# Batch 0's down-sampled attention in blocks of 128 and 16 queries, with four smaller edits around it

## Chip, core and metric

The kernel runs on one core of one Trainium2 chip. The metric is the device time of one execution in microseconds; the median of several runs is given. A core has TensorE (PE in the profile: matmuls; PEld are its weight loads), VectorE (DVE), ScalarE (ACT), GpSimd (POOL) and SyncE (SP), each with its own queue of instructions in program order. Semaphores order them against each other and against the DMAs.

## What is computed

Two stages. The first is attention over inputs `q`, `k`, `v` of shape (8 batches, 8 heads, 576 positions, 64). For each batch and head two attentions are added: one over means of four neighbouring positions (144 of them, its output repeated four times), and one in which a query sees only keys less than four positions away:

```python
q_d = q.reshape(B, H, Sd, factor, D).mean(axis=3)      # k_d, v_d alike; factor 4, Sd 144
out_d = sm_attn(q_d, k_d, v_d)
out_up = np.repeat(out_d, factor, axis=2)
mask = np.abs(pos[:, None] - pos[None, :]) < factor
scores = np.where(mask, scale * np.matmul(q, k.transpose(0, 1, 3, 2)), -1000000000.0)
out_local = np.matmul(softmax(scores), v)
return out_up + out_local
```

(`softmax` stands here for the five lines of the reference that spell it out.) The second stage takes the result as `x`, 4608 tokens of 512 values, through two matrix products with a gate between them:

```python
h = x @ w_in                                           # w_in 512 x 2048
g = h * (1.0 / (1.0 + np.exp(-1.702 * h)))
return (g @ w_out).astype(np.float32)                  # w_out 2048 x 512
```

## The kernel before

**Tiles and stages.** The second stage is cut into nine groups of 512 tokens. A group has `mm1` (16 blocks of 128 columns of `w_in`, four matmuls each, line L703, then a Silu on ScalarE, L714) and `mm2` (64 matmuls, L759, or a split form for the last tokens). The attention of batch g + 1 is cut into steps, and the lists `POS` and `POS_0` name the block of group g before which each step is issued on TensorE; `POS_0` is for group 0, whose steps belong to batch 1, and `VDP_0` places `prep_vd_pe(1, ...)`. So attention and matrix products share TensorE in an order written out by hand; nothing is scheduled automatically.

**The start.** Batch 0's attention has nothing to hide behind. It is a straight list of calls after line L797: loads, constants, `warm` (matmuls of zeros in fp32, L656; each appears in the trace as two records), `scores` (L384) and `scores_d` (L403, down-sampled) of two quads of heads, their exponentials on ScalarE (`exp_local` L414, `exp_down` L420), then for each of four head pairs `av_local0` (L523), `av_down0` (L539) and `normalise0` on VectorE (L558 to L565), then `transp_sum` (L580 and L591), which transposes the result and adds the up-sampled part, and `copy_x` (L604 to L610) into `xT`. The partial products of group 0's first six column blocks (`part`, L703) stand between the transposes.

**Sums of v.** Batch 0's down-sampled values are made on TensorE by `prep_vd_pe` (L346) in three chunks: the first two with one copy on ScalarE (L355), the third with another. The third is issued after `scores_d(0, 1, PA[2])`; so ScalarE has that copy, and then `exp_down(1, sd)`, in its queue. PSUM tile `PA[2]` holds the second down-scores until `exp_down` has read them, and is then the output tile of the third head pair.

**`av_down0`** takes, for each head pair, ten blocks of up to 64 queries, each for two heads: 20 matmuls with 48 rows (positions), 64 columns of weights and 65 columns of values (64 and a column that sums). Down-sampled queries 0 to 47, 48 to 95 and 96 to 143 lie in three places of the output tile.

**`up`** is a 0/1 matrix by which `transp_sum` repeats each down-sampled query four times. It is made of a difference of indices (iotas on GpSimd, L113 to L116) by Abs and Exp on ScalarE (`make_up`), with a bias that `make_bias` computes on VectorE. `mask` (used for batches 1 to 7 at L428) is spread out on ScalarE by `make_mask` after the third head pair.

**Queues.** GpSimd's queue issues most loads (q, k, v of batches 0 and 1, the weights) and does iotas, sums and memsets between them. A wait at one of these holds all that is behind it. After the start it holds, in this order: `load_w_out(1)`, the memset of `v4` (L888), `load_vb(1, 0)`, `load_vb(1, 1)`, the pooling of batch 1. SyncE issues the loads of later batches and the stores.

Of the kernel before, what the change touches and what calls it, by code (L numbers as in the profile page):

```python
# [8 lines left out]
FP32 = mybir.dt.float32  # L9
BF16 = mybir.dt.bfloat16  # L10
AF = mybir.ActivationFunctionType
# [8 lines left out]
def kernel(  # L20
# [9 lines left out]
    nc = tc.nc  # L30
    B, H, S, D = q.shape
    SD = S // 4
# [14 lines left out]
    consts = ctx.enter_context(tc.tile_pool(name="consts", bufs=1))  # L47
    persist = ctx.enter_context(tc.tile_pool(name="persist", bufs=1))
# [7 lines left out]
    id128 = consts.tile([128, 128], BF16, name="id128")  # L56
# [4 lines left out]
    vbs = [persist.tile([128, 5, H, 65], BF16, name=f"vb{i}") for i in range(2)]  # L61
    vds = [persist.tile([128, 3, HP, 65], BF16, name=f"vd{i}") for i in range(2)]
    es = [persist.tile([128, 2, 304], BF16, name=f"es{i}") for i in range(4)]
    eds = [persist.tile([128, 2, 464], BF16, name=f"ed{i}") for i in range(2)]
    v4 = persist.tile([128, 3, HP, 4 * D], FP32, name="v4")
    kdT = [persist.tile([128, 160, 2], BF16, name=f"kdT{i}") for i in range(NQ)]

# [1 line left out]
    PM = [psum.tile([128, 512], FP32, name=f"pm{i}") for i in range(2)]  # L69
# [9 lines left out]
        turn["m"] += 1  # L79
        return PM[turn["m"] % 2]  # L80

    UP = 120
    wz = consts.tile([128, 512], FP32, name="wz")
    off = consts.tile([128, 60], BF16, name="off")
    psel = consts.tile([128, 7, 64], BF16, name="psel")
# [5 lines left out]
    di = consts.tile([128, 128], FP32, name="di")  # L91
    dr = consts.tile([128, 1], FP32, name="dr")
    du = consts.tile([128, UP], FP32, name="du")
    bias = consts.tile([128, 4], FP32, name="bias")
    dp = consts.tile([128, 7, 64], FP32, name="dp")
    it = dict(allow_small_or_imprecise_dtypes=True)
    halves = [slice(0, 64), slice(64, 128)]
# [13 lines left out]
        nc.gpsimd.iota(di, pattern=[[-1, 128]], base=0, channel_multiplier=1, **it)  # L111

    def iota_up():  # L113
        for par in range(2):
            nc.gpsimd.iota(du[halves[par]], pattern=[[1, UP]], base=-48 * par,
                           channel_multiplier=-1, **it)  # L116

    def fill():
        nc.vector.memset(wz, 0.0)
        for t in kdT:  # L120
            nc.vector.memset(t[:, SD:160, :], 0.0)
        for t in vbs:
            nc.vector.memset(t[:, :, :, 64:65], 1.0)
        for t in vds:
            nc.vector.memset(t[:, :, :, 64:65], 4.0)
        for t in es:
            nc.vector.memset(t[:, :, 300:304], 1.0)
        for t in eds:
            nc.vector.memset(t[:, :, 432:464], 1.0)


    def make_off():
# [4 lines left out]
        )  # L137

    def make_mask():
        nc.scalar.copy(  # L140
            out=mask.rearrange("p x (i c) -> p (x i) c", c=60),
            in_=dm[:, None, :].to_broadcast([128, 10, 60]),
        )
# [5 lines left out]
        nc.vector.tensor_single_scalar(out=id128, in_=di, scalar=0.0, op=ALU.is_equal)  # L149

    def make_bias():
        nc.vector.memset(bias[:, 3:4], -3.0)
        nc.vector.reduce_sum(
            out=bias[:, 2:3], in_=id128.rearrange("p (h c) -> p h c", h=2)[:, :, 0:48],
            axis=mybir.AxisListType.XY,
        )
        nc.vector.tensor_copy(out=bias[:, 0:2], in_=rv)
        nc.vector.tensor_scalar(
            out=bias[:, 0:3], in0=bias[:, 0:3], scalar1=-1.0, scalar2=400.0,
            op0=ALU.add, op1=ALU.mult,  # L160
        )

    def make_up():
        nc.scalar.activation(out=du, in_=du, func=AF.Abs)
        nc.scalar.activation(
            out=up, in_=du[:, :, None].to_broadcast([128, UP, 4]),
            func=AF.Exp, scale=-400.0, bias=bias[:, 2:3],
        )

    rv = consts.tile([128, 2], FP32, name="rv")  # L170
# [14 lines left out]

    def end_psel():
        nc.scalar.activation(out=dp, in_=dp, func=AF.Abs)
        nc.scalar.activation(out=dp, in_=dp, func=AF.Relu, bias=bias[:, 3:4])
        for sl, c in ((slice(0, 1), 1), (slice(1, 7), 0)):
            nc.scalar.activation(  # L190
                out=psel[:, sl], in_=dp[:, sl],
                func=AF.Exp, scale=-400.0, bias=bias[:, c : c + 1],
            )
# [201 lines left out]
    def scores_d(b, qd, sd=None):  # L395
        sd = sd or ps_tile()
        bank = banks(sd)
        for kc in range(3):
            for a in range(2):
                for r in range(4):  # L400
                    rows = slice(32 * r, 32 * r + 32)
                    j = r % 2
                    nc.tensor.matmul(  # L403
                        bank[r // 2][64 * j : 64 * j + 64, SD * kc : SD * kc + SD],
                        lhsT=kdT[qd][rows, 48 * kc : 48 * kc + 64, a],
                        rhs=qdT[b, qd][rows, :, a],
                        start=(a == 0), stop=(a == 1),
                        tile_position=(32 * r, 64 * j),
                    )
        return sd  # L410
# [119 lines left out]

    def av_down0(hp, o):
        Ed, vd, u = eds[hp // 2], vds[0], hp % 2
        blocks = [(0, 3)] + [(kc, c) for kc in range(3) for c in (0, 1)]
        blocks += [(kc, 2) for kc in range(3)]
        for kc, c in blocks:
            pos, slot = ((0, 6), (1, 6), (1, 4), (1, 5))[c]
            for j in range(2):
                q0 = SD * kc + 48 * c if c < 3 else 0
                nc.tensor.matmul(  # L539
                    o[64 * pos : 64 * pos + 64, j, 65 * slot : 65 * slot + 65],  # L540
                    lhsT=Ed[64 * j : 64 * j + 48, u, q0 : q0 + 64],
                    rhs=vd[64 * j : 64 * j + 48, kc, hp, :],
                    start=(kc == 0), stop=(kc == 2 or c == 3),
                    tile_position=(64 * j, 64 * pos),
                )

    def y_tiles0():
        return (
# [20 lines left out]

    def transp_sum(y, x):  # L570
        y, yd = y[:2]
        ups = [
            (0, 6, sub(x[0], 3, (1, 228)), sub(up, 3, (228, 2), (1, 114))),
            (0, 6, sub(x[0], 0, (1, 3)), sub(up, 0, (1, 3))),
            (0, 4, sub(x[0], 231, (1, 117)), sub(up, 267, (1, 117))),
            (1, 6, sub(x[1], 3, (1, 228)), sub(up, 117, (228, 2), (1, 114))),
            (1, 4, sub(x[1], 156, (1, 75)), sub(up, 192, (1, 75))),
        ]
        for n, (bank, slot, to, what) in enumerate(ups):
            nc.tensor.matmul(  # L580
                to, lhsT=yd[:, slot // 2 - 2, :, :], rhs=what,
                start=n in (0, 3), stop=True,
                skip_group_check=True,
            )
# [14 lines left out]
        return x  # L599
# [53 lines left out]
    def warm(n, cols=512, t=None):  # L653
        t = pm_tile() if t is None else t
        for _ in range(n):
            nc.tensor.matmul(  # L656
                t[:, 0:cols], lhsT=wz[:, 0:128], rhs=wz[:, 0:cols], start=True, stop=True
            )

    def attention(b, slots=None):  # L660
        st = {}
# [124 lines left out]
            f()  # L786

    POS = [13, 16, 33, 42, 53, 62, 71]
    POS_0 = [16, 18, 27, 46, 50, 55, 64, 68, 73]
    VDP_0 = 41  # L790

    o, y, x = {}, {}, {}

# [33 lines left out]
    prep_1("q", 0, 1)  # L827
    reduce_qk(0, 1, "k")
    reduce_qk(0, 1, "q")
    warm(3)  # L830
    exp_down(0, scores_d(0, 0, PA[2]))
    make_up()
    sp = scores(0, 1, barred=True, sp=PA[0:2])
# [6 lines left out]
    for hp in range(2):  # L840
        av_local0(hp, o[hp], range(4))
        normalise0(o[hp], y[hp], "a")
    sd = scores_d(0, 1, PA[2])
    prep_vd_pe(0, PM[1], range(2, 3))
    exp_down(1, sd)
    nc.scalar.preload_act_table_set("silu_and_others")
    for hp in range(3):
        av_local0(hp, o[hp], range(4 if hp < 2 else 0, 5))
        av_down0(hp, o[hp])
        normalise0(o[hp], y[hp], "b" if hp < 2 else "ab")  # L850
    warm(1, t=PM[0])
    make_mask()

    gT0 = new_gT()
# [103 lines left out]
```

## Time and profile before

| | |
|---|---|
| median of 5 runs | 328.76 us (325.86 to 330.29) |
| the profiled execution, its own time | 328.37 us |
| its span, first to last instruction | 326.4 us |
| mean granted TensorE clock | 0.990 |
| VectorE, ScalarE, GpSimd busy | 41%, 57%, 43% of the span |
| matmuls of the second stage, L703 and L759 | 121.5 and 121.7 us busy |
| first scores matmul (L384), first partial product (L703), end of the partial products | 8.35, 26.36, 33.6 us |
| group 1's first `mm1` matmul | 66.3 us |

The profile is of one execution. Its page gives, for each engine, the share of the span in which it was busy, the chain of work that ended last, and the costliest groups of instructions by line. The trace behind it can be asked for the waits of an engine (which instruction waited, and for whom), for the instructions in order of time, and for the busy times and the granted TensorE clock in any stretch. "<-issue" means that the profile shows nothing that the instruction waited for. Time in which an engine other than the bounding one idles costs nothing by itself.

### The profile page before, as it was taken

The page shows a single profiled execution, that of the slowest core. Times are in us where ns is not written, and L with a number is a line of the kernel's source. Part 1 is how long each engine was busy: PE and PEld are TensorE (multiplying, and loading weights), DVE is VectorE, ACT ScalarE, POOL GpSimd, SP SyncE. Part 2 cuts the span into 40 slices and gives each one's busy share as a digit, 9 for nine tenths or more (in the row PEclk, how much of TensorE's full clock was granted, in tenths as well). Part 3 has the DMA queues.
Part 4 walks back from the last instruction along what each step waited for, and adds up shares of the span by engine and source line. Part 5 has one row for each costly group of instructions (what it writes and reads, how often), then busy time and mean ns, then how long its engine had stood idle before and what let it go on. Part 6 is the DMA issues. An engine that isn't in the chain of part 4 may idle for free.

```text
span 326.4 us, 11056 instructions
## 1 busy us (share of the span) xinstructions
PE 316.1 (97%) x4954; PEld 158.2 (48%) x4954; DVE 132.9 (41%) x221; ACT 185.1 (57%) x321; POOL 139.0 (43%) x171
## 2 busy tenths in 40 slices
PE   8979979999999999999999999999999999999996
PEld 3545444445554555455544554455444544444444
DVE  6864422760477037803681277226730560000000
ACT  4443873465936593559366746674567556415611
POOL 8983950069505960497029801990098000000000
PEclk9978999999999999999999999999999999999999
DMA  7999999989716991599139922995190100021012
GB/s 124 122 195 210 165 139 214 186 216 184 147 50 150 194 192 39 145 197 204 44 98 222 182 86 89 186 205 109 66 145 3 68 34 34 0 75 56 0 55 74
DMA packets 63550, 40.02 MB, mean 123 GB/s; under 512 B 44048, under 2 KB 54416, under 8 KB 63504
## 3 DMA queue, kind: packets, MB, share of 16 engines
q1 hardware_dynamic: 44496, 24.32, 34.6%
q0 software_dynamic: 18864, 14.95, 31.9%
q8 instruction: 38, 0.62, 0.8%
q14 instruction: 8, 0.07, 0.1%
q10 hardware_dynamic: 144, 0.07, 0.1%
HBM read 44.83 MB, written 9.44 MB: 166 GB/s over the span
## 4 chain that ended last, share of the span: by engine, by line
PE 91%; DMA 2%; issue 2%; POOL 2%; ACT 1%; DVE 1%; POOLq 0%; DVEq 0%
PE pm L703 36%; PE pm L759 36%; PE pa L384 3%; PE pa L703 2%; DMA qb<-in_q_dram 2%; PE pa L759 2%; PE pa L403 2%; PE pa L498 2%; PE pa L445 2%; PE pa L467 2%; PE pm L774 1%; DVE y L484 1%; POOL vb L233 1%; PE pm L656 1%; PE pa L508 0%
## 5 line engine op out<-in xcount | busy, mean ns | idle before, releaser
L759 PE MATMUL pm<-w_out_bf,gT 128*128 128x512 bf16 x528 | 121.7, 380 | 0.0
L703 PE MATMUL pm<-xT,w_in_bf 128*128 128x512 bf16 x544 | 121.5, 380 | 0.0
L714 ACT ACTIVATE gT<-pm 128x512 bf16<-128x512 f32 x136 | 81.1, 598 | 44.9 <-PE pm L703 44.8
L703 PEld LDWEIGHTS <-w_in_bf 128*128 128x128 bf16 x576 | 55.7, 98 | 66.8 <-issue 0.4
L759 PEld LDWEIGHTS <-gT 128*128 128x128 bf16 x560 | 51.5, 98 | 59.1 <-issue 0.2
L428 DVE TENSOR_TENSOR es<-es,mask 128x600 bf16<-128x600 bf16 x28 | 19.9, 725 | 92.0 <-ACT es L414 91.2
L309 POOL TENSOR_TENSOR pq<-kT 128x576 f32<-128x576 bf16 x14 | 16.2, 1156 | 95.2 <-DVE kT L279 95.2
L744 ACT ACTIVATE osb<-pm 128x512 f32<-128x512 f32 (+2 forms) x35 | 20.8, 593 | 40.2 <-PE pm L759 36.4
L617 ACT COPY od<-pa 128x384 f32<-128x384 f32 (+1 forms) x56 | 18.5, 412 | 30.8 <-DVE y L484 22.4
L484 DVE TENSOR_TENSOR y<-pa,rc 128x896 bf16<-128x896 f32 x28 | 30.6, 1092 | 1.0
L638 DVE TENSOR_TENSOR xT<-pa,od 128x570 bf16<-128x570 f32 x28 | 21.1, 753 | 10.6 <-ACT od L617 9.8
L746 DVE TENSOR_SCALAR osb<-pm 128x128 f32<-128x128 f32 x1 | 0.3, 292 | 55.3 <-ACT osb L744 55.3
L325 POOL TENSOR_TENSOR v<-v 112x512 f32<-112x512 f32 x18 | 22.8, 1264 | 0.0
L414 ACT ACTIVATE es<-pa 128x600 bf16<-128x600 f32 x32 | 19.7, 667 | 2.8 <-PE pa L384 2.6
L279 DVE STREAM_TRANSPOSE kT<-kb 128x576 f32<-128x576 f32 x16 | 19.9, 1246 | 0.0
L279 DVE STREAM_TRANSPOSE qT<-qb 128x576 f32<-128x576 f32 x16 | 19.8, 1237 | 0.0
L233 POOL DMA_DIRECT2D vb<-in_v_dram x20 | 13.7, 702 | 6.5 <-DMA w_in_bf<-in_moe_w_in_dram 4.0
L420 ACT ACTIVATE ed<-pa 128x864 bf16<-128x864 f32 x16 | 14.4, 897 | 3.7 <-PE pa L403 3.7
L384 PEld LDWEIGHTS <-kT 32*64 32x64 bf16 x1280 | 11.7, 104 | 6.7 <-issue 5.3
L309 POOL TENSOR_TENSOR pq<-qT 128x576 f32<-128x576 bf16 x13 | 14.9, 1146 | 0.0
L483 DVE RECIPROCAL rc<-pa 128x14 f32<-128x14 f32 x28 | 6.7, 240 | 19.9 <-PE pa L467 19.9
L328 POOL TENSOR_TENSOR vd<-v 112x256 bf16<-112x256 f32 x18 | 13.6, 758 | 1.4
(97 smaller groups left out, 270.4 us busy)
## 6 DMA issues: line engine op xcount, KB each, us to landing
out_dram<-osb SPq DMA_DIRECT2D x35, 256.0 KB, 2.1
vf<-in_v_dram SPq DMA_DIRECT2D x60, 128.0 KB, 5.8
v<-in_v_dram SPq DMA_DIRECT2D x36, 192.0 KB, 4.9
kb<-in_k_dram POOLq DMA_DIRECT2D x16, 288.0 KB, 6.9
qb<-in_q_dram POOLq DMA_DIRECT2D x16, 288.0 KB, 8.2
w_out_bf<-in_moe_w_out_dram POOLq DMA_DIRECT2D x4, 512.0 KB, 13.1
vb<-in_v_dram POOLq DMA_DIRECT2D x20, 64.0 KB, 5.5
w_in_bf<-in_moe_w_in_dram POOLq DMA_DIRECT2D x2, 512.0 KB, 7.0
```

The lines of the kernel that those rows point to most:

```text
L279: nc.vector.transpose(out=t32.rearrange("p (i c) -> p c i", c=18), in_=store[b, qd].bitcast(FP32).rearrange("p (c d) -> p c d", c=18),)
L309: nc.gpsimd.tensor_tensor(out=t1, in0=sv[:, :, 0:2, :], in1=sv[:, :, 2:4, :], op=ALU.add)
L325: eng.tensor_tensor(out=t1[0:112], in0=x[:, :, 0:2, :], in1=x[:, :, 2:4, :], op=ALU.add)
L384: nc.tensor.matmul(sp[r // 2][64 * par : 64 * par + 64, r % 2, 60 * i : 60 * i + 60], lhsT=kT[b, qd][rows, k0 : k0 + 64, a], rhs=qT[b, qd] ...
L414: nc.scalar.activation(out=es[2 * qd + u][:, :, 0:300], in_=sp[u][:, :, 0:300], func=AF.Exp, scale=inv_sqrt_d,)
L428: nc.vector.tensor_tensor(out=ev, in0=ev, in1=mask, op=ALU.mult)
L484: nc.vector.tensor_tensor(out=y[:, xs], in0=ov[:, :, :, 0:D], in1=rc[:, xs].to_broadcast([128, n, 7, D]), op=ALU.mult,)
L638: eng.tensor_tensor(out=sub(xT[hp], t0 + 3, (57, 2), (114, 5), (1, 57)), in0=sub(x, 3, (509, 2), (57, 5), (1, 57)), in1=sub(od, 3, (57, 2) ...
L703: nc.tensor.matmul(acc, lhsT=w_in_bf[:, dmc, ffc * 128 : (ffc + 1) * 128], rhs=xT[dmc][:, g * TG : g * TG + TG], start=(dmc == 0), stop=(d ...
L714: nc.scalar.activation(out=gT[:, ffc, :], in_=acc, func=AF.Silu, scale=GELU_SCALE)
L744: eng.activation(out=osb, in_=ap, func=AF.Copy, scale=1.0 / GELU_SCALE)
L759: nc.tensor.matmul(ops[t], lhsT=gT[:, ffc, t * 128 : (t + 1) * 128], rhs=w_out_bf[:, ffc, :], start=(ffc == 0), stop=(ffc == n_ffc - 1),)
```

## The change

`av_down0` takes 128 queries in one block and the last 16 in another: 12 matmuls for 20. The second block's values are repeated, so that one matmul with 130 columns fills two slots of the output. The layout of `up`, its iotas, the bias and the five up-sampling matmuls of `transp_sum` follow. The third chunk of `prep_vd_pe` is issued before the second `scores_d`. `make_mask` runs on GpSimd. The three fp32 warming matmuls before the first `scores_d` become 22 bf16 matmuls with 256 columns, and the fp32 warming matmul after the third head pair is removed. Batch 1's steps from the fourth on are placed two blocks later, and `VDP_0` three.

```diff
-    UP = 120
+    UP = 144
...
     def iota_up():
-        for par in range(2):
-            nc.gpsimd.iota(du[halves[par]], pattern=[[1, UP]], base=-48 * par,
-                           channel_multiplier=-1, **it)
+        nc.gpsimd.iota(du[:, 0:128], pattern=[[1, 128]], base=0,
+                       channel_multiplier=-1, **it)
+        nc.gpsimd.iota(du[:, 128:UP], pattern=[[1, UP - 128]], base=64,
+                       channel_multiplier=-1, **it)
...
     def make_mask():
-        nc.scalar.copy(
+        nc.gpsimd.tensor_copy(
...
     def make_bias():
-        nc.vector.memset(bias[:, 3:4], -3.0)
-        nc.vector.reduce_sum(
-            out=bias[:, 2:3], in_=id128.rearrange("p (h c) -> p h c", h=2)[:, :, 0:48],
-            axis=mybir.AxisListType.XY,
-        )
+        nc.vector.memset(bias[:, 2:3], -3.0)
...
         nc.scalar.activation(
             out=up, in_=du[:, :, None].to_broadcast([128, UP, 4]),
-            func=AF.Exp, scale=-400.0, bias=bias[:, 2:3],
+            func=AF.Exp, scale=-400.0,
         )
...
     def av_down0(hp, o):
         Ed, vd, u = eds[hp // 2], vds[0], hp % 2
-        blocks = [(0, 3)] + [(kc, c) for kc in range(3) for c in (0, 1)]
-        blocks += [(kc, 2) for kc in range(3)]
-        for kc, c in blocks:
-            pos, slot = ((0, 6), (1, 6), (1, 4), (1, 5))[c]
-            for j in range(2):
-                q0 = SD * kc + 48 * c if c < 3 else 0
-                nc.tensor.matmul(
-                    o[64 * pos : 64 * pos + 64, j, 65 * slot : 65 * slot + 65],
-                    lhsT=Ed[64 * j : 64 * j + 48, u, q0 : q0 + 64],
-                    rhs=vd[64 * j : 64 * j + 48, kc, hp, :],
-                    start=(kc == 0), stop=(kc == 2 or c == 3),
-                    tile_position=(64 * j, 64 * pos),
-                )
+        for p0, n, q0, slots in ((0, 128, 0, (6, 7)), (64, 64, 128, (4, 6))):
+            for kc in range(3):
+                for j in range(2):
+                    c0, c1 = 65 * slots[0], 65 * slots[1]
+                    nc.tensor.matmul(
+                        o[p0 : p0 + n, j, c0:c1],
+                        lhsT=Ed[64 * j : 64 * j + 48, u, SD * kc + q0 : SD * kc + q0 + n],
+                        rhs=vd[64 * j : 64 * j + 48, kc, hp, None, :].to_broadcast(
+                            [48, slots[1] - slots[0], 65]
+                        ),
+                        start=(kc == 0), stop=(kc == 2),
+                        tile_position=(64 * j, p0),
+                    )
...
             (0, 6, sub(x[0], 0, (1, 3)), sub(up, 0, (1, 3))),
-            (0, 4, sub(x[0], 231, (1, 117)), sub(up, 267, (1, 117))),
+            (0, 6, sub(x[0], 231, (1, 53)), sub(up, 459, (1, 53))),
+            (0, 4, sub(x[0], 284, (1, 64)), sub(up, 512, (1, 64))),
             (1, 6, sub(x[1], 3, (1, 228)), sub(up, 117, (228, 2), (1, 114))),
-            (1, 4, sub(x[1], 156, (1, 75)), sub(up, 192, (1, 75))),
...
+    zero16 = wz.bitcast(BF16)[:, 0:256]
...
-    POS_0 = [16, 18, 27, 46, 50, 55, 64, 68, 73]
-    VDP_0 = 41
+    POS_0 = [16, 18, 27, 48, 52, 57, 66, 70, 75]
+    VDP_0 = 44
...
     reduce_qk(0, 1, "q")
-    warm(3)
+    for n in range(22):
+        nc.tensor.matmul(
+            PM[1][:, 0:256], lhsT=zero16[:, 0:128], rhs=zero16, start=True, stop=True
+        )
     exp_down(0, scores_d(0, 0, PA[2]))
...
+    prep_vd_pe(0, PM[1], range(2, 3))
     sd = scores_d(0, 1, PA[2])
-    prep_vd_pe(0, PM[1], range(2, 3))
     exp_down(1, sd)
...
         normalise0(o[hp], y[hp], "b" if hp < 2 else "ab")
-    warm(1, t=PM[0])
     make_mask()
```

The tiles `eds` grow from 464 to 480 columns, and the columns that `fill` sets to 1 with them.

More of the change, by code (lines that the diff above doesn't have):

```diff
@@ L63 @@
     es = [persist.tile([128, 2, 304], BF16, name=f"es{i}") for i in range(4)]
-    eds = [persist.tile([128, 2, 464], BF16, name=f"ed{i}") for i in range(2)]
+    eds = [persist.tile([128, 2, 480], BF16, name=f"ed{i}") for i in range(2)]
     v4 = persist.tile([128, 3, HP, 4 * D], FP32, name="v4")
@@ L93 @@
     du = consts.tile([128, UP], FP32, name="du")
-    bias = consts.tile([128, 4], FP32, name="bias")
+    bias = consts.tile([128, 3], FP32, name="bias")
     dp = consts.tile([128, 7, 64], FP32, name="dp")
@@ L128, in fill @@
         for t in eds:
-            nc.vector.memset(t[:, :, 432:464], 1.0)
+            nc.vector.memset(t[:, :, 432:480], 1.0)
     def make_off():
@@ L151, in make_bias @@
     def make_bias():
-        nc.vector.memset(bias[:, 3:4], -3.0)
-        nc.vector.reduce_sum(
-            out=bias[:, 2:3], in_=id128.rearrange("p (h c) -> p h c", h=2)[:, :, 0:48],
-            axis=mybir.AxisListType.XY,
-        )
+        nc.vector.memset(bias[:, 2:3], -3.0)
         nc.vector.tensor_copy(out=bias[:, 0:2], in_=rv)
         nc.vector.tensor_scalar(
-            out=bias[:, 0:3], in0=bias[:, 0:3], scalar1=-1.0, scalar2=400.0,
+            out=bias[:, 0:2], in0=bias[:, 0:2], scalar1=-1.0, scalar2=400.0,
             op0=ALU.add, op1=ALU.mult,
@@ L187, in end_psel @@
         nc.scalar.activation(out=dp, in_=dp, func=AF.Abs)
-        nc.scalar.activation(out=dp, in_=dp, func=AF.Relu, bias=bias[:, 3:4])
+        nc.scalar.activation(out=dp, in_=dp, func=AF.Relu, bias=bias[:, 2:3])
         for sl, c in ((slice(0, 1), 1), (slice(1, 7), 0)):
@@ L581, in transp_sum @@
                 to, lhsT=yd[:, slot // 2 - 2, :, :], rhs=what,
-                start=n in (0, 3), stop=True,
+                start=n in (0, 4), stop=True,
                 skip_group_check=True,
```

## The prediction

> **What bounds the kernel now.** I read the page first, then the waits of TensorE, its timeline, and the busy times and clock by stretches.
>
> ```profile
> span 326.4 us, 11056 instructions
> ...
> PE 316.1 (97%) x4954; PEld 158.2 (48%) x4954; DVE 132.9 (41%) x221; ACT 185.1 (57%) x321; POOL 139.0 (43%) x171
> ...
> q8 instruction: 38, 0.62, 0.8%
> ```
>
> TensorE is the bound: busy 97% of the span and 91% of the chain that ended last. From 66 us on the chain is almost only its matmuls. Whatever the change brings must come from the first 66 us. Who does TensorE wait for there?
>
> ```profile
> PE pa L403 <- issue: 2.3, 1, 2.3
> PE pa L539 <- issue: 1.5, 1, 1.5
> ```
>
> Columns: us in total, times, longest. These are the two large waits, and both are "issue": no semaphore ended them. The timeline of TensorE shows the second one and what follows:
>
> ```profile
> 18.51 0.40 PE L539 MATMUL pa<-vd,ed 48*64 48x65 bf16 x20
> 19.16 0.35 PE L523 MATMUL pa<-vb,es 64*64 64x65 bf16 x19 [0.25 <-ACT ed L420]
> ...
> 19.35 0.22 PE L539 MATMUL pa<-vd,ed 48*64 48x65 bf16 x3
> 21.10 0.49 PE L539 MATMUL pa<-vd,ed 48*64 48x65 bf16 x15 [1.53 <-issue]
> 21.52 2.07 PE L656 MATMUL pm<-wz 128*128 128x512 f32 x2
> 23.39 0.78 PE L580 MATMUL pm<-up,yd 128*128 128x228 bf16 x5
> ```
>
> TensorE stops five matmuls into `av_down0` of the third head pair, with all operands there, stands from 19.57 to 21.10, runs the other 15, then the warming matmul (L656), then `transp_sum`. The stretches (TensorE busy and count, weight loads, VectorE, ScalarE, GpSimd, granted clock, DMA share, GB/s):
>
> ```profile
> 17.24:20.65 3.41, 1.86 (x97) 1.23 (x89) 2.93 (x9) 2.68 (x4) 2.98 (x5) 1.00 1.16 181
> 20.65:27.48 6.83, 6.38 (x92) 3.71 (x92) 3.07 (x6) 2.19 (x7) 2.72 (x2) 0.50 1.14 212
> 44.55:47.96 3.41, 2.30 (x95) 1.24 (x92) 1.42 (x3) 2.88 (x5) 0.80 (x2) 1.00 1.17 178
> ```
>
> After the stop the clock is 0.50 until 27.5. The stop thus costs its 1.53 us and half the speed of 6.83 us after it.
>
> [...]queue q8 moved 38 packets, 0.62 MB, 16 KB each[...]. Counting matmul records from 0, the two waits end at record 351 and at 735: 384 apart, three blocks of 128 matmuls. [...]these two cost 1.53 and 2.25 us. The packet records of q8 show how: TensorE entered the block before (record 223) at 16.22, the packet ran from 18.23 to 19.60, matmuls resumed 1.50 later. For record 735: entered at 42.77, packet 46.86 to 47.80, resumed 1.31 later. So a block comes 2.0 to 4.1 (queueing[...]) + 0.9 to 1.6 (packet) + 1.5 us after the previous one is entered, and stops TensorE when its 128 small matmuls take less. [...]0.50 for 6.83 us, two windows, after one that was 55% busy; the stretch from 44.55, 67% busy, kept 1.00.
>
> **The change part by part.** *Counts of instructions.* Up to the stop the change adds 22 bf16 matmuls, removes the three fp32 ones (six records) and removes eight in each of the two `av_down0` before it: 22 - 6 - 16 = 0. The boundary stays five matmuls into the third `av_down0`. But the one before it, record 223, comes after the warming (+16) and ahead of any `av_down0`: it moves from the first `av_local0` (16.22) to the second half of the next `warm(1)`, about 14.2. The fetch that was late is asked for 2.0 us earlier. With the same 2.0 + 1.4 + 1.5 it is usable at 19.1; the boundary is reached at about 19.2 (below). I take it that the stop goes; the bounds are queueing of 0.6 us (usable 17.7) and 4.1 us (21.2, stop as before).
>
> *Third sum chunk ahead of the down-scores.* Four L346 matmuls (0.36 us) go before 24 of L403 (0.51). Their data, the last `vb` transfer, landed at 16.27, before 16.98 where they now start. The ACT queue has CAST `vd` (17.95 to 18.33) and then exp (18.21 to 19.11) in the same order; now the cast runs about 17.45 to 17.8, while TensorE does L403, and exp 17.95 to 18.85: 0.26 us earlier. Behind exp wait the third `av_local0` (bank `PA[2]`) and the table load. The four L346 delay L403 by 0.36, less than the cast took away.
>
> *`av_down0`.* 20 matmuls become 12 with 1170 columns for 1300. Batch 1's four heads' worth of the same kind, 80 matmuls (lines L445 and L467), ran from 60.76 to 61.33, so 8 fewer are 0.06 us; [...]I take 0.05 gained. `transp_sum`: five as before, 576 columns for 651, 0.03 us each at full clock.
>
> *Mask.* ACT loses 0.69 us at 20.42, where it then idles to 24.61. On GpSimd a cast of 2560 elements took 2.34 us, so 600 take 0.55; the two-input 576 took 1.15: 0.5 to 1.2 us. Behind it in the POOL queue: memset `v4` (2.65 us), one `vb` issue at 23.15, then a wait of 4.0 us until 27.86 for a `w_in` DMA. The cover is that wait; VectorE reads the mask only at 44.89. Cost 0.
>
> *Warming.* Six fp32 records ran from 9.12 to 11.89. 512 columns of bf16 take 0.216 us (0.43 a pair), so 22 of 256 take 2.4; L403 waits for `qdT` (VectorE, 11.67) anyway. [...]The fp32 warming at 21.52 goes: -2.00 us[...].
>
> *Small ones.* Iotas 0.22 + 0.24 become about 0.25 + 0.14 (rows L111, L110), -0.07; `make_up` does 576 columns for 480, +0.1 by the row of 600 in 0.67. Together 0, on the path (exp of scores at 15.46). The reduce on VectorE (0.25) and larger memsets lie beside waits for `kb`, `qb`: 0.
>
> *After the stop.* Walking TensorE on at full clock: third pair done 19.45; `transp_sum` 0 (0.97 at half clock, now 0.55) to 20.0; fourth pair to 20.5; `transp_sum` 1 to 21.05; the first partial matmuls wait for ACT's copies (table load ends 20.1, then 0.98 a copy), 0.15; `transp_sum` 2 waits for VectorE's third normalise (21.85), 0.2; `transp_sum` 3 for the fourth (23.43), 0.4; the remaining 18 at 0.216. The end of the partial matmuls moves from 33.61 to 27.9. Cross-check: 1.53 + 2.00 + half of 4.4 us of work at half clock + 0.26 + 0.2 - 0.75 of these waits = 5.4. I take 5.5.
>
> *Will batch 1's data be there?* Landings (from the records): last `w_in` 27.57, `qb` of batch 1 30.4 and about 33, `w_out` parts 35.7, 38.7, 48.9, 50.8, last `vb` 44.36. Needed after the change: ffc 8 at 29.6, down-scores at 37.0 (GpSimd's sums end 35.8), second part at 39.4, `vb` at 46.4 (three steps later than now), third at 49.3. All fit, by 0.4 to 2 us. The moved steps cost 0.1: the last merge then ends 0.05 before its reader, now 0.48.
>
> *The stop at 49.11.* Its boundary (18 records later in the program) falls behind two L759, 0.56 later than now after the previous one: 2.25 becomes 1.7, with queueing from 1 to 4.1 us 0 to 2. Take -0.5.
>
> **Sum:** 5.5 + 0.5 - 0.1 = 5.9. Span 326.4 - 5.9 = 320.5; the profiled execution's time is 1.97 above its span, so 322.5; it lay 0.4 below the median of the runs (328.76), so 322.8.
>
> **Rivals.** *Half clock anyway (16%)*: the stop goes, but TensorE still idles near 15.6, 16.6 and 18.6 (0.27 + 0.23 + 0.4)[...]. Against: that is under 35% of 3.41, and 33% idle was borne at 44.55. Loss up to half of 6.83 less waits that it fills: 2.9, so 325.7. *The stop stays (14%)*: queueing of 4 us at record 223. Then only the warming is won, 2.00 less what the half clock eats of it later, 0.86 to 1.4 with the rest: 327.5. *Slower (10%)*: one mechanism, at record 95. Its crossing moves from 10.51 to about 9.4, record 223 from 16.22 to 14.2; the block must be usable by 14.2, so its packet must start by 11.3. Above 1.9 us of queueing (0.62 was measured there) TensorE stops there too; at 4.1 it stands 2.3 us, enters the next block at 16.5, stops at 351 until 21.5 to 23[...]: +3, 331.5. *The change does nothing* would need the wait not to be the fetch; the 384 speaks against it, and I count that under the second.
>
> **Chances.** Main case 60%: 322.8, from 319.8 (no stop at 735 either, 2 us, and the runs' own scatter) to 325. The range takes in the first two rivals: 319.8 to 327.8, leaving out the slower case and a little. Over 1% (3.3 us, about what can be told from no change) faster: 0.60 + half of 0.16 + some of the second = 0.72; within 0.18; slower 0.10.
>
> **What would show it.** No "issue" wait at L539; a q8 packet starting near 16 and not 18.2; clock 1.00 from 20 to 28; exp of the second down-scores ending near 18.85; the partial matmuls ending near 28; 1 to 2 us still lost near 43, now at L759. Wrong: a q8 packet that starts after 17.5, a clock of 0.50 anywhere, TensorE waiting for `vb` or `w_out` of batch 1.

## The result, and the profile after

The changed kernel took 325.15 us (median of 43 runs, 321.8 to 330.07); the kernel before, run beside it on the same chips, 326.2 us (80 runs, 323.67 to 331.06). The ratio is 0.9954 with a 95% interval from 0.9936 to 0.9971: 1.5 us faster where 5.9 us were forecast. (The ratio leaves out, for both kernels, the runs that took over 1.5% more than the fastest one; the two medians are of all runs, and lie 1.05 us apart.) 322.8 was the forecast time; 325.15 lies inside the stated range, but the size of the change is a quarter of the forecast. And the kernel before itself came out at 326.2, 2.6 us below the median of the five runs that the forecast started from (the 80 take these five in).

The profiled execution took 325.43 us, 2.9 less than the profiled one of before. Its page:

```profile
span 323.7 us, 11019 instructions
...
PE 315.9 (98%) x4936; PEld 159.3 (49%) x4936; DVE 134.0 (41%) x220; ACT 184.4 (57%) x320; POOL 139.5 (43%) x172
...
q8 instruction: 38, 0.62, 0.8%
```

18 matmuls fewer (16 more in the warming, 32 fewer in `av_down0`, the two records of the late warming gone), as counted. The waits of TensorE (us in total, times, longest):

```profile
PE pa L464 <- issue: 1.1, 1, 1.1
PE pa L442 <- issue: 0.6, 1, 0.6
PE pa L534 <- issue: 0.5, 1, 0.5
```

The wait in `av_down0` (now L534) shrank from 1.5 to 0.5, and the 2.3 of batch 1's down-scores is gone. But two others have come: 1.1 us in batch 1's products (L464, at 58.7 us) and 0.6 us in those of a later batch (120 us). The timeline of TensorE around the third head pair:

```profile
18.92 0.26 PE L534 MATMUL pa<-vd,ed 48*128 48x65 bf16 x5
19.72 0.48 PE L534 MATMUL pa<-vd,ed 48*128 48x65 bf16 x7 [0.54 <-issue]
20.13 0.45 PE L577 MATMUL pm<-up,yd 128*128 128x228 bf16 x5
```

The stop is again five matmuls into `av_down0`, at record 351, and `transp_sum` follows at once, without the warming. The stretches (columns as before the change; the granted clock is the third figure from the end):

```profile
13.97:17.38 3.41, 2.90 (x72) 1.53 (x70) 2.29 (x6) 2.88 (x6) 3.41 (x8) 1.00 1.16 122
17.38:20.79 3.41, 2.87 (x95) 1.99 (x85) 2.94 (x9) 2.27 (x3) 1.10 (x2) 1.00 1.20 193
20.79:27.62 6.83, 6.83 (x87) 3.80 (x83) 2.62 (x5) 2.60 (x9) 4.74 (x4) 0.50 1.13 212
```

Here is the surprise: after 3.41 us in which TensorE was 84% busy by the trace the clock was 0.50 all the same, for 6.83 us, as before. (The trace's complete records of the granted clock last 13.653, 6.827 and 296.960 us here, 13.653, 6.827 and 300.373 before: 4, 2, 87 and 88 times 3.413. A 3.413 us piece of them is called a window.) The end of the partial products came at 31.7 us, not at 27.9.

**The granted clock sorts the runs.** Each run's mean clock is given with its time, and it takes steps: 1.000, 0.995, 0.989, 0.984. One window of 3.41 us at half clock is half of 3.41 in 324, or 0.005, so each step is taken for one such window (the profiled execution, with 6.83 us at 0.50, has a mean of 0.989). Counting them so (203 runs of the kernel before, from three sessions of the experiments below, without the 27 of a fourth, one of which took 528.23 us at a clock of 0.56; 44 of the changed kernel):

| half-clock windows in a run | before: share, median us | changed: share, median us |
|---|---|---|
| 0 | 28%, 324.8 | 36%, 323.2 |
| 1 | 39%, 326.3 | 23%, 324.8 |
| 2 | 30%, 329.3 | 32%, 326.0 |
| 3 or more | 3%, 331.3 | 9%, 329.1 |

The profile that the prediction was read from was one with two windows. From two windows to none is 329.3 to 323.2, 6.1 us, close to the 5.9 that were forecast. But the change doesn't take the windows away (1.2 a run after, 1.1 before); it is worth 1.6 us in runs without them and 3.3 in runs with two. Nor is the clock all that these runs differ in: two windows at half clock can take at most 3.4 us, and the kernel before is 4.5 us slower with two than with none. What the rest is stays open.

### The profile page after: what moved, and what is told of

Same layout as the page of the kernel before. It is cut to its first block, busy times and chain, and to the rows that moved or that the text cites. A ratio compares the mean times of both kernels' runs of the same rounds, so it can differ in the third digit from the quotient of the medians.

```text
span 323.7 us, 11019 instructions
## 1 busy us (share of the span) xinstructions
PE 315.9 (98%) x4936; PEld 159.3 (49%) x4936; DVE 134.0 (41%) x220; ACT 184.4 (57%) x320; POOL 139.5 (43%) x172
## 4 chain that ended last, share of the span: by engine, by line
PE 91%; DMA 2%; ACT 2%; POOL 2%; issue 1%; DVE 1%; POOLq 0%; DVEq 0%
PE pm L702 37%; PE pm L758 35%; PE pa L381 3%; PE pa L702 2%; PE pa L758 2%; DMA qb<-in_q_dram 2%; PE pa L400 2%; PE pa L442 2%; PE pa L495 2%; PE pa L464 2%; PE pm L773 1%; ACT es L411 1%; PE pa L534 1%; POOL vb L230 1%; PE pa L577 1%
## 5 line engine op out<-in xcount | busy, mean ns | idle before, releaser
L306 POOL TENSOR_TENSOR pq<-kT 128x576 f32<-128x576 bf16 x14 | 16.2, 1158 | 89.8 <-DVE kT L276 89.8
## 6 DMA issues: line engine op xcount, KB each, us to landing
w_out_bf<-in_moe_w_out_dram POOLq DMA_DIRECT2D x4, 512.0 KB, 14.2
```

Source lines behind the costliest of these rows:

```text
L306: nc.gpsimd.tensor_tensor(out=t1, in0=sv[:, :, 0:2, :], in1=sv[:, :, 2:4, :], op=ALU.add)
```

## Experiments

Theories: the half-clock windows come from the stop for an instruction block (*stop*, the prediction's), or from how little of the array the small matmuls use (*array use*), and the prediction's profile was one *draw* among several. Then: which parts of the change carry the 1.6 us. Each kernel was timed in five rounds unless said otherwise. Records are matmuls counted from 0. In the trace of before the first twelve packets of q8 (16,384 bytes each, the page's "instruction") start 0.62 to 4.09 us after records 95, 223, 351 and so on, every 128, and its two long issue waits end at 351 and 735; these records are called the boundaries of instruction blocks.

### b_again: the kernel before once more

No edit.

> The kernel before, unchanged, profiled once more. Theory 'draw': the waits for instruction blocks at records 351 and 735 and the half-clock windows differ from execution to execution, and the profile that the prediction was made from was a bad one. Then this profile has other lengths for the two waits (sum clearly below the 3.8 us of before), and the granted clock of its runs falls into steps of about 0.005 (one window of 3.41 us at half clock is 1.7 of 325), with times that follow: about 324 without a window, 326 with two. Theory 'fixed': the two waits are again 1.5 and 2.3 us and nearly all runs have a clock of 0.990.

Median 325.82 us (22 runs), ratio 0.9992 (0.9962 to 1.0023); 9 runs had no window, 7 one, 4 two, 2 three. This profile is of a run at full clock, and its waits are others:

```profile
PE pa L539 <- issue: 1.2, 1, 1.2
PE pa L467 <- issue: 1.0, 2, 0.8
PE pa L384 <- DVE qT L279: 0.9, 1, 0.9
PE pa L445 <- issue: 0.5, 1, 0.5
```

1.2 us at record 351 and, at 735, 0.16 where the first profile had 2.25; instead 0.8 and 0.5 at records 863 and 991. With the 1.2 us at 351 the clock stayed at 1.00 here. So 'draw' holds: two executions of one kernel waited 1.5 and 1.2 us at the same record 351, and 2.25 and 0.16 at 735. What is missing at 735 stands at 863 and 991, where the first profile had no wait; that the one leads to the other is not shown.

### a_latewarm: the late warming put back

```diff
         normalise0(o[hp], y[hp], "b" if hp < 2 else "ab")
+    warm(1, t=PM[0])
     make_mask()
```

> The changed kernel with the fp32 warming matmul after the third head pair put back (two records). Theory 'the warming was pure cost': 0.9 us slower than the changed kernel at full clock, up to 2.0 in half-clock runs, and the clocks spread as in the changed kernel. Rival 'it holds the clock': a run has fewer half-clock windows with it (more runs at 1.0), and the median is no slower than the changed kernel's 325.2.

Median 326.35 (22 runs). In the nine runs without a window 323.94, 0.76 above the changed kernel's 323.18; windows 1.5 a run, so it doesn't hold the clock. Its price in the changed kernel is near what its two records take at full clock (0.96 us from their start to that of the next matmul, in this profile), less than half of the 2.00 that the prediction read off a half-clock profile.

### a_fp32: three fp32 warmings for the 22 bf16 ones

```diff
-    for n in range(22):
-        nc.tensor.matmul(
-            PM[1][:, 0:256], lhsT=zero16[:, 0:128], rhs=zero16, start=True, stop=True
-        )
+    warm(3)
```

> The changed kernel with the three fp32 warming matmuls in place of the 22 bf16 ones: 16 records fewer ahead of everything. Theory 'block boundary': record 223 falls 16 records later in the program (into the first local product, about 15.9 us instead of 14.2), its fetch starts about 1.7 us later, and record 351 (now the last records of the third head pair, or behind it) is waited for 1.5 to 2.2 us instead of 0.5. Later boundaries move too. Rival 'the warming only warms': the wait stays at 0.5 us, and the time is that of the changed kernel within 0.3 us.

The boundaries moved as counted: record 223 was crossed at 16.22 us in the first local product, and 351 fell into `transp_sum` (L588) at 20.53. But the wait there was 0.17 us, not 1.5 to 2.2: the packet came 2.05 us after the crossing, took 0.97, and matmuls resumed 1.28 later, while the later boundary was itself reached 1.2 us later (20.36 for 19.19). A miss in size. The time without windows, 323.26 (11 of 16 runs), is the changed kernel's. So the bf16 warming brought no gain that can be seen. It may even cost windows: with the fp32 matmuls there were 0.44 a run for 1.2, and the median of all runs is 323.60, a ratio to before of 0.9919 (0.9890 to 0.9949), where the changed kernel has 0.9954 (0.9936 to 0.9971). The intervals overlap and the sessions differ, so this is a hint and not a result.

### a_busy, a_small, a_busy4: full and small matmuls ahead of the third head pair

```diff
     for hp in range(3):
+        if hp == 2:
+            for n in range(8):
+                nc.tensor.matmul(
+                    PM[0][:, 0:256], lhsT=zero16[:, 0:128], rhs=zero16,
+                    start=True, stop=True,
+                )
         av_local0(hp, o[hp], range(4 if hp < 2 else 0, 5))
```

`a_small` has `lhsT=zero16[0:32, 0:64], rhs=zero16[0:32, :]` into 64 partitions instead, as many matmuls of as many columns on an eighth of the array. `a_busy4` has four of the full ones.

> The changed kernel with eight bf16 zero matmuls (128 x 128 weights, 256 columns, 0.87 us of the full array) before the third head pair, where TensorE waits for the exponential. By the trace TensorE was 84% busy in the window before the clock fell (17.4 to 20.8), so busy time by the trace doesn't decide. Theory 'array use': [...]the head pairs' 64 x 65 tiles count little (about 0.2 of the window), and with 0.87 us of full matmuls added it stays above what it stayed above from 44.5 us on. Then nearly all runs have a clock of 0.995 to 1.0, the profile shows 1.00 from 20.8 to 27.6, and the time is 1 to 2 us below the changed kernel's median in spite of 0.5 us more on TensorE. Theory 'stop': the clock falls because TensorE stands at record 351 (now inside these eight matmuls or just after them); then the clocks spread as in the changed kernel, and the time is 0.5 us above it.

> The control of a_busy: the same eight matmuls of 256 columns in the same place, but with 32 rows and 64 columns of weights, an eighth of the array; as many records, as long in time. Theory 'array use': the clock falls as in the changed kernel (about 1.2 windows a run, a third of the runs without any), median about 325. Theory 'time busy' (TensorE must only be kept running, with whatever): as a_busy, nearly all runs at full clock, median 323.4.

> a_busy with four matmuls instead of eight, 0.43 us of the full array. Theory 'array use' with a threshold: between a_busy (0.05 windows a run) and the changed kernel (1.2); I expect 0.2 to 0.7 windows, median 323.2 to 324.2. If already four hold the clock in nearly all runs, the median is at most a_busy's 323.4, as they end before the exponential that the third pair waits for.

| | runs | without a window | windows a run | median us | median without windows |
|---|---|---|---|---|---|
| changed kernel | 44 | 16 | 1.2 | 325.0 | 323.2 |
| a_small | 24 | 10 | 1.25 | 325.1 | 322.8 |
| a_busy4 | 16 | 14 | 0.12 | 322.9 | 322.9 |
| a_busy | 20 | 19 | 0.05 | 323.4 | 323.1 |

(The changed kernel's row has one run, of 324.4 us, more than the 43 above; hence 325.0.) The control decides: with the same time on TensorE (1.06 and 1.05 us for the eight, in the two profiles) there were 1.25 windows a run with the small tile and 0.05 with the full one. Keeping TensorE running wasn't enough here.

Where do the windows lie in a profile? The records of the clock start and change whole multiples of 3.413 us apart (the lengths above), so each profile's windows can be counted from its own. They lie differently in each: one begins at 17.38 us in the profile of the changed kernel, at 18.48 in that of `a_busy4`. The windows of `a_busy4` around the head pairs:

```profile
15.07:18.48 3.41, 2.86 (x86) 1.87 (x83) 2.07 (x5) 2.97 (x6) 3.41 (x7) 1.00 1.08 152
18.48:21.90 3.42, 3.42 (x105) 2.48 (x98) 3.01 (x9) 2.34 (x4) 1.81 (x3) 1.00 1.22 205
21.90:25.31 3.41, 3.36 (x55) 2.13 (x53) 1.78 (x4) 1.97 (x9) 3.30 (x2) 1.00 1.12 213
```

of `a_small`'s profiled run:

```profile
16.20:19.57 3.37, 3.13 (x102) 2.14 (x97) 2.41 (x7) 2.86 (x5) 2.70 (x6) 1.00 1.21 195
19.57:22.98 3.41, 2.17 (x47) 1.64 (x45) 1.13 (x5) 0.57 (x1) 3.35 (x3) 1.00 1.19 214
22.98:29.60 6.62, 6.40 (x83) 3.63 (x82) 3.03 (x6) 2.60 (x9) 2.43 (x4) 0.50 1.11 211
```

and of `b_again`, the kernel before in a run at full clock:

```profile
15.71:19.12 3.41, 2.78 (x135) 1.97 (x134) 2.54 (x7) 2.60 (x5) 2.65 (x5) 1.00 1.16 180
19.12:22.54 3.42, 2.28 (x72) 1.50 (x71) 2.51 (x7) 1.76 (x3) 3.38 (x2) 1.00 1.17 199
```

In `a_small`'s profile TensorE also stood 1.24 us at record 351, in the window before the fall, so that profile alone doesn't tell 'stop' from 'array use'; the counts of runs do.

An estimate of array use, worked out from the traces: a matmul's columns at 0.216 us for 512 (the rate of L703), times rows and weight columns over 128 x 128. Up to 66 us the windows at full clock after which the clock fell had 0.28 (changed kernel, from 17.4), 0.20 (before), 0.19 (`b_nowarm`), 0.18 and 0.07 (`a_small`) and 0.12 (`b_pos`). The lowest after which it stayed had 0.28 (`a_busy4_pos_c`, from 16.2), 0.29 (`a_latewarm`) and 0.30 (`b_again`); those of `a_busy4` and `a_busy` had at least 0.35 and 0.46. By this estimate the two groups meet at 0.28 in these profiles; that the clock goes by it is not shown. The share of time that TensorE is busy doesn't sort them: 84% fell, while 67% (`b_again` from 19.1, use 0.46) and 61% (`a_busy4_pos` from 54.0, use 0.34) stayed. Two things beside it. In `b_again` the 3.41 us from 17.05 have 0.18, less than some after which the clock fell elsewhere, and it stayed; an edge at 19.12 cuts them in two, so where the windows lie may count too. And the stop lowers the estimate: without idle time (16%, 0.54 us of it the stop) the changed kernel's window would have had 0.28 / 0.84 = 0.33. So by the estimate the stop can be part of it where it falls into a window of small tiles; it was not taken away by itself.

`a_busy4`'s 322.9 is the lowest median here: ratio to before 0.9925 (0.9900 to 0.9949), against 0.9954 (0.9936 to 0.9971) for the change alone. It beats the kernel before; against the changed kernel the intervals overlap. (In three variants of `a_busy4` below 0.7 to 0.8 windows a run remained, and one of them, `pos`, is the same program up to batch 1's steps. Whether four are too few or the session counts is open.)

### b_busy: the same eight in the kernel before

> The kernel before with the eight full-array bf16 matmuls ahead of the third head pair and nothing else of the change. Theory 'array use': nearly all runs at 0.995 to 1.0, median about 325.1, which is 1.5 below before, from the clock alone; the stop at record 351 (now inside the third head pair's first products) stays about 1 us long, so a stop doesn't make the clock fall. Theory 'stop': windows as frequent as before, median 326.5 or more.

Median 325.28 (22 runs), 17 of them without a window, 0.32 windows a run against 1.0 of before; 0.96 us below before's 326.24, at the predicted level, but with a ratio of 0.9977 (0.9951 to 1.0003) not clear of nothing. So 17 of 22 runs kept the clock without the change. Record 351, now in L523, had a wait of only 0.24 us in its profile, not the 1 us expected, so this run doesn't tell whether a long stop alone would lower the clock.

### b_nowarm, b_busy4_nowarm: the late warming alone

```diff
-    warm(1, t=PM[0])
     make_mask()
```

`b_busy4_nowarm` has this and four full matmuls ahead of the third head pair.

> The kernel before without the fp32 warming matmul after the third head pair, nothing else changed. Theory 'its own length': 0.8 us less than before in runs at full clock (about 324.1 for 324.9), 1.5 to 2 less in runs with two half-clock windows, and the windows are as frequent as before (about 1.1 a run). Rival 'it holds the clock': more windows than before, median as before or slower. If the first holds, this one edit is half of what the change brought at full clock (1.7 us); the rest would be the earlier exponential, the shorter products and the moved block boundary.

> With the clock held by four full-array matmuls ahead of the third head pair, the parts of the change can be priced without the clock. This is the kernel before with these four and without the late fp32 warming. Theory 'the warming is 0.86 us of TensorE': 0.9 below b_busy at full clock (324.87), so about 324.0, and nearly all runs without a half-clock window. Rival 'given back': the time is that of b_busy, 324.9, because a stop for an instruction block (record 735 or 863) becomes longer by what is saved ahead of it, as in b_nowarm.

Neither gained. `b_nowarm`: 326.26 (14 runs), 324.98 in its four runs without windows; before had 324.35 there. It had 1.43 windows a run, where before had 1.02: that is what 'it holds the clock' asked for, but 14 runs are few, the share without windows is the same (29% and 31%), and `a_latewarm` points the other way (1.5 with the warming, 1.2 without). `b_busy4_nowarm`: 324.84 in seven such runs, where `b_busy` has 324.87, the rival's figure; 1.14 windows a run, so here four matmuls didn't hold the clock, a miss. Why is open: its one profile, with a stop of 1.1 us at 351, is at full clock. Is the warming's time given back at the boundaries? The timeline of TensorE, first of `b_busy4_nowarm`, then of `b_busy` (start, length, instruction, and the idle time before it):

```profile
20.82 0.39 PE L539 MATMUL pa<-vd,ed 48*64 48x65 bf16 x19 [1.12 <-issue]
...
44.35 0.51 PE L403 MATMUL pa<-qdT,kdT 32*64 32x144 bf16 x18 [0.98 <-issue]
```

```profile
20.00 0.22 PE L523 MATMUL pa<-vb,es 64*64 64x65 bf16 x2 [0.24 <-issue]
43.74 0.58 PE L403 MATMUL pa<-qdT,kdT 32*64 32x144 bf16 x24 [0.55 <-issue]
```

At record 351 TensorE stood 1.12 us in the first and 0.24 in the second. But this boundary lies ahead of the warming's place, so the warming can't be the reason; the four full matmuls fewer can. Behind it, at 735, it stood 0.98 and 0.55 us, having come there at 43.37 and 43.19. So these two profiles show waits that differ by 0.88 and 0.43 us, as much as the warming takes or half of it, and not where its time went.

### a_busy4_order, a_busy4_av20, a_busy4_pos: parts of the change undone

Each undoes one part in `a_busy4`. `order`:

```diff
-    prep_vd_pe(0, PM[1], range(2, 3))
     sd = scores_d(0, 1, PA[2])
+    prep_vd_pe(0, PM[1], range(2, 3))
```

`av20` has the old `av_down0` with its `up`, iotas, bias and up-sampling products. `pos`:

```diff
-    POS_0 = [16, 18, 27, 48, 52, 57, 66, 70, 75]
-    VDP_0 = 44
+    POS_0 = [16, 18, 27, 46, 50, 55, 64, 68, 73]
+    VDP_0 = 41
```

> a_busy4 with the third sum chunk behind the second down-scores again, as before. Theory of the prediction: the second exponential ends 0.26 us later (about 18.8 instead of 18.5), the third head pair starts 0.26 later, and the time is 323.2, 0.26 above a_busy4's 322.94. Rival: nothing, 322.9, as the copies on ScalarE and the normalising on VectorE set the pace behind it.

> a_busy4 with av_down0 in 20 matmuls again, and with it the old up, iotas, bias and up-sampling products; the rest of the change stays. Theory of the prediction: 8 matmuls more in each of four head pairs cost 0.05 us each, and the block boundary falls 16 records earlier in the third pair (into its first products): 0.2 us slower at most, 323.1. Rival 'wide blocks are slow': in the trace of the changed kernel the four av_down0 took about 0.4 us each at full clock, more than the 20 small ones, so the old form is as fast or faster, 322.5 to 322.9.

> a_busy4 with batch 1's steps at their old places (two or three blocks earlier). Prediction's price of the move: 0.1 us for it. Theory 'it gives the data time': prep_vd_pe of batch 1 is issued near 46.0 and waits for the last vb transfer (landing 44.4 to 45.9) or for ScalarE, and the stops for blocks come closer together: 0 to 1 us slower, 323.0 to 323.9. Rival: 0.1 faster, 322.8.

| against a_busy4, runs without windows | runs | median us | difference |
|---|---|---|---|
| a_busy4 | 14 | 322.93 | |
| order | 15 | 323.23 | +0.3 |
| av20 | 12 | 323.94 | +1.0 |
| pos | 13 | 325.00 | +2.1 |

`a_busy4` ran in another session than the three; the kernel before had 324.35 without windows in its session and 324.76 in theirs, so some 0.4 of each difference may be the session's. `order` is then not told from nothing, `av20` costs 0.6 to 1.0 and `pos` 1.7 to 2.1, both above what was expected of them. For `av20` its one profile suggests why. The small tiles are not slow (20 took 0.40 us in the profile of before, at 18.51; 12 wide ones 0.56 in that of `a_busy4`, at 18.66), but there are 32 more of them, and two boundaries were waited for:

```profile
PE pa L580 <- issue: 1.4, 1, 1.4
PE pa L523 <- issue: 1.0, 1, 1.0
```

Records 351 and 479 are waited for by 1.0 and 1.4 us; the second is a boundary that lies 32 matmuls later in the program of `a_busy4`, behind partial products of 0.216 us each, and is passed there without a wait. If so, the wide blocks pay by their count.

### b_pos, a_busy4_vdp, and two more profiles of a_busy4_pos

`b_pos` has the new places alone in the kernel before; `a_busy4_vdp` is `a_busy4` with `VDP_0 = 41` only; `a_busy4_pos_b` and `a_busy4_pos_c` are `a_busy4_pos` profiled again.

> The kernel before with batch 1's steps at the new places (POS_0 and VDP_0) and nothing else. In a_busy4 the old places cost 2.1 us in runs without a half-clock window (325.0 against 322.9), where the prediction had a loss of 0.1 for the new ones. Theory 'the moved steps are the gain': 1.5 to 2 us less than before at full clock (about 323.0 for 324.7), windows as frequent as before. Rival 'only once the rest is early': batch 1's data is late only for a kernel that gets there sooner, so in the kernel before the move brings nothing (324.4 to 325.0).

> a_busy4 with VDP_0 alone at its old place (41 for 44), POS_0 new. Theory 'vb lands late': the sums of batch 1 (prep_vd_pe) wait for the last vb transfer in most runs and hold TensorE; then this one place costs most of the 2.1 us, about 324.5 at full clock. Rival 'spacing': what costs is where the products and transposes fall against the block boundaries and data of w_out; then this is 322.9 to 323.3.

> The kernel a_busy4_pos once more, for a second profile: its first profile was of its fastest execution (322.96), which doesn't show where 325.0 comes from. Theory 'vb lands late': a wait of 0.5 to 2 us at prep_vd_pe of batch 1 (L343) for a vb DMA. Rival 'blocks': issue waits at L464 or L442 with a sum of 2 us or more, where a_busy4 has 0.9.

> The same for a third profile: which of the two waits is there, and whether it is there in both.

`b_pos`: 326.06 (22 runs), ratio 1.0004 (0.9975 to 1.0032); 324.37 without windows (5 runs), before 324.16 (4 runs). The new places bring the kernel before nothing. `a_busy4_vdp`: 323.12 without windows (5 runs), so the place of `prep_vd_pe` by itself isn't it. Both further executions took 324.4 at full clock. The third profile's waits, and the place of the one for `vb` in its timeline:

```profile
PE pa L464 <- issue: 1.5, 2, 1.0
...
PE pm L343 <- DMA vb<-in_v_dram: 1.0, 1, 1.0
PE pa L442 <- issue: 0.7, 2, 0.4
```

```profile
16.81 0.30 PE L343 MATMUL pm<-vb,psel 128*64 128x256 bf16 x2 [0.99 <-DMA vb<-in_v_dram]
```

The second profile has 1.4, 0.5 and 0.7 there, the first 1.3, none and 0.6; `a_busy4` has 0.9 at L464, 0.2 at L442 and no `vb` wait. The wait for `vb` is at 16.81 us (15.97 in the second profile): it is for batch 0's values, long before the moved steps, and `order`, with the new places, has one of 0.7 there too. No profile of the old places has a wait for batch 1's `vb`, so nothing speaks for 'vb lands late'. The waits at L464 and L442 sum to 2.1 and 2.2 us in the two further profiles, as 'blocks' asked, and to 1.9 in the first; that is 0.8 to 1.1 more than `a_busy4`'s, half of what was to be explained, and in part in later batches, whose steps are at the same places in both kernels. From the start of batch 1's scores to group 1's first `mm1` matmul the three profiles took 22.68, 23.69 and 22.61 us, and `a_busy4` 22.80: only one of them loses anything where the steps were moved. So the difference of 1.7 to 2.1 us is measured between sets of runs, and its cause is open.

## Why the prediction was wrong, step by step

**The base.** The costs of one execution were taken for the kernel's. That execution had two half-clock windows and block waits of 3.8 us; of 203 runs of before 30% have two windows, 28% none. The working measured its sum against the profile's own time and carried it over to a median of five runs that lay 2.6 us above that of all 80. The single page, with its mean clock of 0.990, couldn't show that other executions differ; the five times (325.86 to 330.29) spread over 1.3%, and the prediction took that for scatter.

**"After the stop": the term that failed.** Of its 5.5 us about 3 were the half clock's (by the prediction's own figures half of 4.4 us of work and half of the warming's 2.07), and they rested on the half clock following from the stop, which its one profile showed as an order in time only: a stop of 1.53 us, then 0.50 for 6.83 us. The prediction took the share of time that TensorE is busy for the measure (55% fell, 67% stayed), so that a shorter stop would keep the clock; that was the author's estimate. It didn't: the changed kernel's window was 84% busy and fell, and half-clock windows are as frequent after as before, 1.2 and 1.1 a run. What the change is worth at the same number of windows is 1.6 us (none) or 3.3 (two). `a_small` against `a_busy` (1.25 and 0.05 windows a run) shows that TensorE's time alone doesn't decide, and the estimate of array use sorts the windows measured here. The rival 'half clock anyway' (325.7, 16%) named the event and nearly the time. Its reason, the idle gaps that are left, may be part of the account (0.54 us of stop were left), but the share of idle time that it went by doesn't sort the windows (16% fell, 33% and 39% stayed).

**The stop at 351.** The count was exact, and so was the start of the fetch: the boundary before it was crossed at 14.20 (forecast about 14.2), the packet began at 16.23, 2.0 us later as assumed; it took 2.07 us instead of 1.4, and matmuls resumed at 19.72 instead of 19.1. 0.54 us of wait remained. The longest wait at a boundary in these profiles is 2.66 us (`a_small`, at the down-scores of batch 1).

**The late warming**, -2.00: at full clock 0.76 in the changed kernel, and nothing in the kernel before; what took it up there isn't shown. The price was the half clock's, and 36% of the changed kernel's runs had no half-clock window to pay it in. (The 0.76 is a difference of two small sets of runs, from different sessions.)

**The stop at 735**, -0.5: in the profile of after it went altogether (-2.25) and 1.15 us came back at record 991. The stops stood at counted records again; the length was not to be had from one profile.

**Down-score order**, -0.26: the exponential ended at 18.52 (forecast 18.85); undoing it cost 0.3 or less, within what two sessions differ by.

**`av_down0`**, -0.2: undoing it costs 0.6 to 1.0, by one profile because of where block boundaries fall and not by its time on the array. The prediction counted instructions up to the first stop and priced the rest by duration alone.

**Batch 1's places**, +0.1: in `a_busy4` the old places cost 1.7 to 2.1 us by the medians, and in the kernel before the new ones bring nothing. The prediction saw in them only the shorter end of group 0; what else they do is open. That batch 1's data would be there "by 0.4 to 2 us" held: TensorE's waits after the change show none for batch 1's `vb` or `w_out`.

**What held, and what was luck.** TensorE bounds (busy 98% of the span after). The changes to mask, iotas and bias cost nothing that shows, though none was run by itself. The walk at full clock was near: it put the end of the partial products at 27.9 us, and at full clock `a_fp32` has 28.8 and `a_latewarm` 29.3. That the time from two windows to none comes to 6.1 us for 5.9 is in part luck: the late warming was priced at 2.00 for 0.76, 0.54 us of the stop stayed, and 1.1 of the 4.5 us by which the two-window runs of before are slower is more than the clock can take.

## What to carry to other kernels

Before a profile is priced, ask how many states its kernel's runs have: here the mean granted clock of each run, in steps of one window, sorted most of a 3% spread, and a sum made from one execution belongs to that execution. Where many small matmuls stand in a row, keep two accounts beside their durations: how many instructions lie between two block boundaries (here 128 matmuls with their loads; the wait at 735 went from 2.25 us to none, and 1.15 came at 991), and how much of the array they use (here eight full-size matmuls in a gap went with full clock in 19 of 20 runs, eight small ones in 10 of 24).

## What was not expected of the hardware

After a stretch of small tiles with TensorE 84% busy the clock was 0.50 for 6.83 us, while with eight full 128 x 128 matmuls (1.05 us) in an existing gap 19 of 20 runs kept it, and with four 14 of 16, though only 40 of 66 runs of three variants. Page and trace of before have 38 instruction packets in the span for 4954 matmuls with as many loads, near every 128th matmul; from a packet's landing to the next matmul took 1.2 to 1.5 us at the four waits of 0.5 us or more in the first 66 us (before and after: records 351, 735; 351, 991), and from a boundary to the start of the packet behind it up to 4.09 us (before, record 607). Executions of one and the same kernel place their block waits differently: 2.25 us at record 735 in one, 0.16 in another.
